# Rows of x scattered to the experts' slots, and TensorE's work in attention grouped by array form

## The chip, the cores and the metric

The kernel runs on one core of a Trainium2 chip. The metric is the device time of one execution in microseconds (us), lower is better. A profile is one execution recorded instruction by instruction; its times are counted from the start of its span. The core's engines are TensorE (PE in the profile, with its weight loads as PEld), VectorE (DVE), ScalarE (ACT), GpSimd (POOL) and SyncE (SP), which issues most transfers. Transfers run on 16 DMA engines. TensorE's clock has two levels, 1.2 and 2.4 GHz; the profile shows the granted clock as a share of the higher.

## The reference

Three layers follow each other. The first is a causal attention with decay, without softmax, over 4 batches of 576 positions and 8 heads of 64. The second is a mixture of 8 experts, each token going to two of them. The third is a dense layer with 2048 hidden units.

```python
scores = scale * np.matmul(q, k.transpose(0, 1, 3, 2))
ret = scores * Dmat                      # gamma_h ** (i - j) for j <= i, else 0
attn = np.matmul(ret, v)
x = attn.transpose(0, 2, 1, 3).reshape(2304, 512)

noisy = x @ w_gate + np.log1p(np.exp(x @ w_noise)) * noise
top2 = two largest of noisy;  top2_w = softmax over the two
out[mask] += top2_w * (np.maximum(x[mask] @ w1[e], 0) @ w2[e])   # for each expert e

h = out @ w_in
return (h * np.clip(h + 3, 0, 6) / 6) @ w_out
```

## The kernel before

Tokens are worked on in 18 tiles of 128 (`NT`). All instructions of an engine run in the order in which the program issues them; the order is written out by hand, and a wait holds everything behind it on the same engine or queue.

**Attention** runs over the tiles `t`. The state over earlier positions is kept as a 64x64 matrix per head (`pS`, copied into `sbd`), so that a tile needs only its own 128 keys. One turn of the loop in `attention` issues, in this order: the loads of tile t+3 on SyncE's queue (`load`, line 165), on some turns a piece of expert weights (`w_load`), the scaling of k and q of tile t+2 on VectorE (`ks`), the scores of tile t+1 on TensorE and their mask on VectorE (`qk`, lines 198 and 200), the gate sums and the rows of x of tile t-1 (`xt`, lines 254 and 259), the store of those rows to the DRAM tensor `xd` (`xstore`, line 221), the transposes of tile t+2 (`tr`, line 183), the output of tile t (`av`, line 211 for its own keys and line 215 for the state), the update of the state (`kv`, line 238), and the gate's logits of tile t-1 (`logit`, line 266).

TensorE's array takes these groups in four forms: line 198 uses half the rows (64x128, two at a time), lines 211 and 238 half the columns (128x64, two at a time), line 254 a quarter of the columns (128x32, four at a time), and lines 183, 215, 259 and 266 the full array (128x128).

**Routing.** Tiles are routed in groups of 4, 4, 4, 3 and 3. `route` is a generator; `rstep` runs its next step, five times in a turn of the loop, so that its short steps on VectorE, ScalarE and TensorE lie between the other work. One step counts with small matmuls (lines 325 to 328) which slot each token has in each of its two experts. The next scatters the tokens' ids with an indirect DMA of GpSimd's, two for each tile (line 344), into `tokd`, a DRAM table with a slot for each row of each expert; the table is filled with zeros at the start (line 140).

**Experts.** `moe` goes through sweeps: a run of an expert's slots against all eight hidden tiles. For each, `ix_load` reads the ids of the slots from `tokd` (line 572, SyncE), and `gather_x` gathers those rows of `xd` with indirect DMAs on GpSimd (line 589). `x_tile` transposes and splits a row tile (line 599), `g1` is the first matmul (line 620), `g2` the second (line 631). The first sweep (expert 0, 360 slots) needs only tokens of the first 12 tiles (`EARLY`); its rows are fetched at turn 15 (`GA`). The second sweep's rows are fetched at its hidden tile 5, when all tokens are routed. The output rows go to `yd`, and `moe2` gathers two for each token and runs the dense layer.

**Buffers.** Tags give rotating buffers: 32 of `big` (tiles of attention and weights), 13 of `row` (rows of x and y), 4 of `xa` (transposed rows of x), 5 accumulators in PSUM.

Of the kernel before, what the change touches and what calls it, by code (L numbers as in the profile page):

```python
# [7 lines left out]
F32 = mybir.dt.float32  # L8
F32R = mybir.dt.float32r
BF = mybir.dt.bfloat16  # L10
I32 = mybir.dt.int32
# [8 lines left out]
NT = N // 128  # L20
# [42 lines left out]
class K:  # L63
# [10 lines left out]
    # slots of one size, shared by all phases  # L74
# [20 lines left out]
    # ---------------------------------------------------------------- setup  # L95
# [23 lines left out]
    def late_consts(self):  # L119
# [11 lines left out]
        self.ids = cp.tile([P, NT], I32, name="ids")  # L131
        nc.gpsimd.iota(self.ids, pattern=[[P, NT]], base=0, channel_multiplier=1)
# [3 lines left out]
        nz = -(-E * REG // P)  # L136
        z = self.row([P, nz], I32)
        nc.gpsimd.memset(z, 0)
# [64 lines left out]
    def av(self, t):  # L203
# [9 lines left out]
        if m:  # L213
            for a in range(4):
                nc.tensor.matmul(px[:, a, :n], self.sbd[t % 2][:, a, :], r["qT"][:, a, :n], start=False,  # L215
                                 stop=True, skip_group_check=True)
        r["xT"] = self.row([P, 4, P])
# [27 lines left out]
    def xt(self, t):  # L245
        """rows of x, and the gate's sums over a quarter of the features each"""
# [4 lines left out]
        o = 256 + t % 2 * P  # L251
        pl = self.pg[:, o:o + P]
        for k in range(4):
            nc.tensor.matmul(pl[32 * k:32 * k + 32, :], self.wgn[:, k, :], r["xT"][:, k, :], start=True, stop=True)
        r["pl"] = self.sb.tile([P, P], F32, name="pl", bufs=2)
        nc.scalar.activation(r["pl"], pl, AF.Copy)
# [3 lines left out]
        r["x"] = self.row([P, DM])  # L260
        nc.scalar.activation(r["x"].rearrange("p (a d) -> p a d", a=4), p, AF.Copy)

    def logit(self, t):
        r = self.raw.pop(t)
        o = t % 8 * 16
        self.nc.tensor.matmul(self.pg[:, o:o + 16], r["pl"], self.c[:, C_FO:C_FO + 16], start=True, stop=True)

    # ---------------------------------------------------------------- route
    def route(self, g0, G):
# [52 lines left out]
        o = 128 + (g0 + 3) // 4 % 2 * 32  # L322
# [17 lines left out]
        for g in range(G):  # L340
            t = g0 + g
            for k in range(2):
# [28 lines left out]
    def late_base(self):  # L371
        """the late tokens of expert 0 start behind its first sweep"""
# [11 lines left out]
    def attention(self):  # L384
        self.raw = {}
# [20 lines left out]
        groups = [(0, 4), (4, 4), (8, 4), (12, 3), (15, 3)]  # L406
        assert EARLY in [g[0] for g in groups]
        self.live, self.sent = [], 0
        for t in range(NT):
# [17 lines left out]
            self.av(t)  # L427
# [5 lines left out]
            if t:  # L433
                self.gate(t - 1, groups)
            self.rstep()
            if t == GA:
                while self.sent < EARLY:
                    self.rstep()
                self.gather_x(0, 0)
            if t in WS:  # L440
                self.w_split()
            self.wstep(WN, eng=self.nc.gpsimd)
        for j in (1, 2):
            self.x_tile(0, xs, j, "acc" if j == 1 else "tp")
        self.xt(NT - 1)
        self.xstore(NT - 1)
# [3 lines left out]
    def gate(self, t, groups):  # L450
        self.logit(t)
# [6 lines left out]
    # ------------------------------------------------- weights, in f order  # L458
    # piece n: expert n // 4, pair of hidden tiles n % 4; from 32 on, moe2's
# [48 lines left out]
    def wstep(self, count=1, until=-1, eng=None):  # L508
        """the next parts of the split; all of piece `until`"""
# [6 lines left out]
    # ------------------------------ float64 weights to float32, chunk by chunk  # L516
# [41 lines left out]
    # ------------------------------------------------------------------ moe  # L558
    # a sweep: an expert's rows in one or two runs of slots, over all hidden tiles
# [3 lines left out]
    def run_of(e, r):  # L563
        """first slot, tiles, rows per tile"""
# [4 lines left out]
    def ix_load(self, e, r, n=1):  # L569
        o, T, R = self.run_of(e, r)  # L570
        t = self.tokd
        self.nc.sync.dma_start(self.ix[r][:R, e:e + n, :], bass.AP(
# [392 lines left out]
```

## Time and profile before

| what | us |
|---|---|
| median of 3 runs | 1035.94 (1035.67 to 1039.35) |
| span of the profiled execution, from its first to its last instruction | 1050.8 |
| what lies around the span in that execution | not listed |
| TensorE matmuls busy in the span | 1011.6 (96%) |
| weight loads | 893.3 (85%) |
| VectorE / ScalarE / GpSimd busy | 506.5 / 413.3 / 241.4 |

The profiled execution's only time is its span, which is 14.9 us longer than the median of the runs. TensorE is busy nearly all of the span, but the span has two parts: attention and routing up to about 205 us, where TensorE has gaps and its clock is at times at the lower level, and the experts and the dense layer behind, where it has next to none. Matmuls are pipelined and their ends are modelled, so starts are the safer measure. "Idle before" is the time for which an engine had nothing running ahead of an instruction, and behind the arrow stands what ended that; "issue" means nothing that the profile shows.

### The profile page before, as it was taken

Reading aid. Unit: us, or ns where it says so; the run is one execution under the profiler, and the core shown is the slowest. Engines: PE = TensorE matmul, PEld = TensorE weight load, DVE = VectorE, ACT = ScalarE, POOL = GpSimd, SP = SyncE. Lnnn points to the kernel's source line nnn. Section 1 sums busy time; section 2 is a strip of 40 time slices with the busy share of each in tenths; the row PEclk is TensorE's granted clock in tenths of the full one; section 3 lists DMA queues with packets and bytes.
Section 4 is the critical chain, followed back from the end, with each engine's and each line's share of the span. In section 5 each row is a group of like instructions: output and inputs, shape, how many; then the busy total and the mean of one; then the engine's idle time right before and its main releaser. Section 6 shows DMA issues by size and latency. Waiting matters only on the chain.

```text
span 1050.8 us, 16775 instructions
## 1 busy us (share of the span) xinstructions
PE 1011.6 (96%) x6370; PEld 893.3 (85%) x6370; DVE 506.5 (48%) x1178; ACT 413.3 (39%) x853; POOL 241.4 (23%) x299
## 2 busy tenths in 40 slices
PE   8988979799999999999999999999999999999996
PEld 5875768699889888898888989999999999999995
DVE  4545545166666666766766256332433333333221
ACT  4434542253434443343434246333433323333322
POOL 0035454402343524352423003110010010000000
PEclk9888879899999999999999999999999999999999
DMA  9878816664374747375545246211010020000000
GB/s 177 190 145 190 163 59 131 193 198 148 124 247 156 252 139 251 124 222 195 162 137 186 80 152 205 65 31 41 11 61 21 19 64 10 31 1 1 31 1 34
DMA packets 130863, 122.04 MB, mean 116 GB/s; under 512 B 68981, under 2 KB 98037, under 8 KB 130773
## 3 DMA queue, kind: packets, MB, share of 16 engines
q1 hardware_dynamic: 123541, 101.32, 34.4%
q0 software_dynamic: 7232, 19.56, 6.3%
q8 instruction: 52, 0.85, 0.4%
q14 instruction: 38, 0.31, 0.1%
HBM read 92.82 MB, written 28.02 MB: 115 GB/s over the span
## 4 chain that ended last, share of the span: by engine, by line
PE 88%; DMA 4%; DVE 2%; SPq 2%; issue 2%; POOL 1%; ACT 0%; another core or an unknown queue 0%; DVEq 0%; POOLq 0%
PE p L631 39%; PE ga L620 21%; PE gb L620 18%; PE xp L599 2%; DMA b<-in_q_dram 2%; PE px L215 1%; PE px L211 1%; SPq L165 1%; DMA b<-in_moe_w_dram 1%; PE sc L198 1%; PE p L183 1%; PE p L238 1%; PE p L259 1%; DMA tokd<-ids,slots 1%; POOL tokd L344 0%
## 5 line engine op out<-in xcount | busy, mean ns | idle before, releaser
L631 PE MATMUL p<-b,h 128*128 128x512 f32 (+1 forms) x1824 | 458.9, 397 | 0.0
L631 PEld LDWEIGHTS p<-b,h 128*128 128x128 f32 (+1 forms) x1824 | 331.4, 187 | 69.7 <-DVE h L668 0.3
L620 PE MATMUL ga<-x,b 128*128 128x360 f32 (+2 forms) x1344 | 235.1, 324 | 1.2 <-DVE h L668 1.2
L620 PEld LDWEIGHTS ga<-x,b 128*128 128x128 f32 x1344 | 218.4, 189 | 9.2 <-DVE h L668 1.9
L620 PE MATMUL gb<-x,b 128*128 128x384 f32 (+2 forms) x768 | 130.1, 318 | 0.0
L620 PEld LDWEIGHTS gb<-x,b 128*128 128x128 f32 x768 | 121.5, 188 | 4.3
L554 POOL TENSOR_TENSOR cvl<-cvl,cva 128x256 f32<-128x256 f32 x64 | 47.2, 738 | 214.8 <-ACT h L667 102.1
L729 POOL DMA_INDIRECT s<-yd,slotc x36 | 35.2, 979 | 253.5 <-DVE s L738 80.7
L620 PE MATMUL gb<-b,b 128*128 128x256 f32 x672 | 89.0, 281 | 0.0
L620 PEld LDWEIGHTS gb<-b,b 128*128 128x128 f32 x672 | 86.2, 189 | 0.5
L513 DVE TENSOR_TENSOR b<-b,b 128x512 fp32r<-128x512 f32 x112 | 79.7, 747 | 12.6 <-ACT b L512 11.9
L789 DVE SCALAR_TENSOR_TENSOR h<-h,h 128x384 fp32r<-128x384 f32 (+1 forms) x112 | 56.1, 501 | 61.1 <-ACT h L788 60.6
L512 ACT ACTIVATE b<-b 128x512 fp32r<-128x512 f32 x128 | 74.5, 623 | 14.9 <-PE p L631 11.9
L788 ACT ACTIVATE h<-h 128x384 fp32r<-128x384 f32 (+1 forms) x112 | 53.7, 479 | 63.7 <-DVE h L787 62.1
L787 DVE SCALAR_TENSOR_TENSOR h<-h,ga 128x384 f32<-128x384 f32 (+1 forms) x56 | 27.8, 497 | 96.3 <-ACT h L786 96.1
L787 DVE SCALAR_TENSOR_TENSOR h<-h,gb 128x384 f32<-128x384 f32 (+1 forms) x56 | 27.8, 497 | 95.4 <-ACT h L786 95.1
L786 ACT ACTIVATE h<-ga,three 128x384 f32<-128x384 f32 (+1 forms) x56 | 30.0, 535 | 99.9 <-PE ga L620 96.5
L786 ACT ACTIVATE h<-gb,three 128x384 f32<-128x384 f32 (+1 forms) x56 | 30.0, 535 | 89.8 <-PE gb L620 88.0
L668 DVE SCALAR_TENSOR_TENSOR h<-gb,h 128x256 fp32r<-128x256 f32 (+1 forms) x64 | 27.9, 435 | 71.5 <-PE p L631 41.2
L667 ACT ACTIVATE h<-ga 128x360 fp32r<-128x360 f32 (+1 forms) x64 | 29.3, 458 | 68.8 <-PE ga L620 66.6
L555 POOL TENSOR_TENSOR cvl<-cvt,cvl 128x256 f32<-128x256 f32 x64 | 54.9, 857 | 5.0
L344 POOL DMA_INDIRECT tokd<-ids,slots x36 | 35.8, 994 | 82.7 <-DVE rs L363 54.2
(129 smaller groups left out, 941.6 us busy)
## 6 DMA issues: line engine op xcount, KB each, us to landing
b<-in_moe_w_dram SPq DMA_DIRECT2D x64, 512.0 KB
s<-in_moe_w_in_dram SPq DMA_DIRECT2D x32, 256.0 KB
s<-in_moe_w_out_dram SPq DMA_DIRECT2D x32, 256.0 KB
yd<-s SPq DMA_DIRECT2D x24, 240.0 KB
xd<-s SPq DMA_DIRECT2D x18, 256.0 KB
out_dram<-s SPq DMA_DIRECT2D x18, 256.0 KB
b<-in_k_dram SPq DMA_DIRECT2D x16, 256.0 KB
b<-in_q_dram SPq DMA_DIRECT2D x16, 256.0 KB
```

Of the source, the lines that this page charges most:

```text
L344: st = nc.gpsimd.indirect_dma_start(out=self.tokd, out_offset=bass.IndirectOffsetOnAxis(ap=self.slots[:, t, k:k + 1], axis=0), in_=self.id ...
L512: self.nc.scalar.activation(h, a, AF.Copy)
L513: (eng or self.nc.vector).tensor_sub(l, a, h.bitcast(F32))
L554: nc.gpsimd.tensor_mul(lf, lf, a.bitcast(F32))
L555: nc.gpsimd.tensor_add(lf, t.bitcast(F32), lf)
L620: nc.tensor.matmul(p, a[:, k, f], b[:, k, :n], start=(i == 0), stop=(i == 11))
L631: nc.tensor.matmul(a[:R], x[:, c], y[:, fi, :], start=(first and i == 0), stop=(last and i == 2))
L729: nc.gpsimd.indirect_dma_start(out=r, out_offset=None, in_=self.yd[0:rows], in_offset=bass.IndirectOffsetOnAxis(ap=self.slotc[:, t, k:k + ...
L786: nc.scalar.activation(r, p, AF.Relu, bias=self.three)
L787: nc.vector.scalar_tensor_tensor(r, r, 6.0, p, op0=OP.min, op1=OP.mult)
L788: nc.scalar.activation(gh, r, AF.Copy, scale=1.0 / 6.0)
L789: nc.vector.scalar_tensor_tensor(gl, r, 1.0 / 6.0, gh.bitcast(F32), op0=OP.mult, op1=OP.subtract)
```

## The change

Two things are changed together.

Rows. The table of ids, its zero fill, the tensor `xd`, its 18 stores, the index loads and the 40 gathers of x go. Instead each tile's 128 rows of x are scattered from SBUF, once for each of the two experts of a token, into `xe`, a DRAM tensor with a 2 KB row for each slot. A sweep reads its rows from there with plain loads on SyncE's queue (`x_load`). The last 128 slots of each expert's first 616, and the last 128 of the first 360, are filled with zero rows at the start, from a tile of zeros.

Order. In a turn of the loop the full-array groups come first (rows of x of tile t-1, logits, transposes of tile t+2, line 215's group of tile t), then the 64-column groups (own keys and state), then the 64-row scores of tile t+1, and on every third turn the gate sums of three tiles at once (`gsum`). The scaling of k and q is issued at the end of a turn, for tile t+3. Routing groups become six of three tiles, and their logits are computed together.

```diff
-        self.tokd = self.dr.tile([P * nz, 1], I32, name="tokd")
-        nc.sync.dma_start(self.tokd.rearrange("(p f) o -> p (f o)", p=P), z)
...
-        self.xd = self.dr.tile([N, DM], F32, name="xd")
+        self.xe = self.dr.tile([E * REG, DM], F32, name="xe")
+
+        z = self.warm.bitcast(F32)
+        nc.sync.dma_start(self.xe.rearrange("(e r) d -> r e d", e=E)[CAP - P:CAP],
+                          z[:, None, :].to_broadcast([P, E, DM]))
+        nc.sync.dma_start(self.xe[NA - P:NA], z)
...
+        if m:
+            for a in range(4):
+                nc.tensor.matmul(px[:, a, :n], self.sbd[t % 2][:, a, :], r["qT"][:, a, :n], start=(a == 0),
+                                 stop=False, skip_group_check=True)
+        self.px = px
+
+    def av2(self, t):
+        nc, m = self.nc, t % 9
+        r, px = self.raw[t], self.px
         for a in range(4):
             for s in range(2):
                 h = slice(s * 64, s * 64 + 64)
-                nc.tensor.matmul(px[h, a, :], r["v"][:, 2 * a + s, :], r["pt"][:, s, a, :], start=(a == 0),
-                                 stop=(m == 0), skip_group_check=True)
...
+                nc.tensor.matmul(px[h, a, :], r["v"][:, 2 * a + s, :], r["pt"][:, s, a, :],
+                                 start=(m == 0 and a == 0), stop=True, skip_group_check=True)
+        g = t // 3
+        if t % 3 == 0:
+            self.xg[g] = self.act_t([P, 4, 3 * P], F32)
+        r["xT"] = self.xg[g][:, :, t % 3 * P:t % 3 * P + P]
         nc.scalar.activation(r["xT"], px, AF.Copy)
-
-    def xstore(self, t):
-        self.nc.sync.dma_start(self.xd[t * P:(t + 1) * P, :], self.raw[t]["x"])
...
+    def gsum(self, g):
+
+        nc = self.nc
+        p = self.pacc([P, 3 * P])
+        x = self.xg.pop(g)
+        for k in range(4):
+            nc.tensor.matmul(p[32 * k:32 * k + 32, :], self.wgn[:, k, :], x[:, k, :], start=True, stop=True)
+        self.pl = self.sb.tile([P, 3 * P], F32, name="pl", bufs=2)
+        nc.scalar.activation(self.pl, p, AF.Copy)
...
-                    out=self.tokd, out_offset=bass.IndirectOffsetOnAxis(ap=self.slots[:, t, k:k + 1], axis=0),
-                    in_=self.ids[:, t:t + 1], in_offset=None)
+                    out=self.xe, out_offset=bass.IndirectOffsetOnAxis(ap=self.slots[:, t, k:k + 1], axis=0),
+                    in_=x, in_offset=None)
...
+        self.ks(2)
+        groups = [(g, 3) for g in range(0, NT, 3)]
...
-            if t + 2 < NT:
-                self.ks(t + 2)
-            if t + 1 < NT:
-                self.qk(t + 1)
+
             if t:
                 self.xt(t - 1)
-                self.xstore(t - 1)
+            if t > 3 and t % 3 == 1:
+                self.gate(t - 2, groups)
             self.rstep()
             if t + 2 < NT:
                 self.tr(t + 2)
+            self.av(t)
             self.rstep()
             self.wstep(WM, eng=self.nc.gpsimd)
-            self.av(t)
+
+            self.av2(t)
             self.kv(t)
             self.rstep()
...
-            if t:
-                self.gate(t - 1, groups)
+            if t + 3 < NT:
+                self.ks(t + 3)
+
+            if t + 1 < NT:
+                self.qk(t + 1)
+            if t and t % 3 == 0:
+                self.gsum(t // 3 - 1)
             self.rstep()
...
+    def x_load(self, e, r):
+
         o, T, R = self.run_of(e, r)
...
+        xv = self.xe[e * REG + o:e * REG + o + T * R].rearrange("(p j) d -> p j d", j=T)
         for j in range(T):
             x = self.row([P, DM])
-            nc.gpsimd.indirect_dma_start(
-                out=x[:R], out_offset=None, in_=self.xd[0:EARLY * P] if (e, r) == (0, 0) else self.xd,
-                in_offset=bass.IndirectOffsetOnAxis(ap=self.ix[r][:R, e, j:j + 1], axis=0))
+            self.nc.sync.dma_start(x[:R], xv[:, j, :])
             self.xr[e, r, j] = x
```

## Rows read from the trace of the kernel before

**Rows 1.** Busy time by stretch: length, each engine's busy time, clock, DMA share, GB/s.

```profile
205.00:1043.30 838.30, 836.33 (x4723) 750.03 (x4721) 412.36 (x874) 331.66 (x673) 169.82 (x193) 1.00 0.34 108
27.40:148.60 121.20, 107.20 (x1183) 87.78 (x1183) 58.50 (x185) 57.50 (x131) 49.12 (x66) 0.87 0.73 156
```

**Rows 2.** TensorE's timeline over one tile: start, length, line, tiles, shape, count.

```profile
37.59 0.69 PE L238 MATMUL p<-b 128*64 128x64 f32 x16
38.20 0.40 PE L266 MATMUL p<-cst,pl 128*128 128x16 f32 x2
38.53 1.16 PE L198 MATMUL sc<-b 64*128 64x128 f32 x16
39.62 0.42 PE L254 MATMUL p<-s,wgn 128*32 128x128 f32 x8
39.98 0.66 PE L259 MATMUL p<-cst,s 128*128 128x128 f32 x4
40.47 1.04 PE L183 MATMUL p<-cst,b 128*128 128x128 f32 x8
41.44 1.09 PE L211 MATMUL px<-b,b 128*64 128x128 f32 x16
42.46 1.10 PE L215 MATMUL px<-b,s 128*128 128x64 f32 x8
43.49 0.68 PE L238 MATMUL p<-b 64*64 64x64 f32 x16
```

**Rows 3.** TensorE's waits, 20 to 150 us: us in total, times, longest.

```profile
PE px L215 <- issue: 4.8, 7, 1.0
PE px L211 <- issue: 3.8, 11, 0.5
...
PE p L238 <- issue: 1.7, 2, 0.9
```

**Rows 4.** GpSimd's indirect DMAs by line: ns shortest, median, longest; first and last start.

```profile
L344 POOL DMA_INDIRECT tokd<-ids,slots x36: 954/958/1297, 55.6 to 179.3; - x36
...
L589 POOL DMA_INDIRECT s<-xd,ixa x24: 973/1016/1457, 143.4 to 575.9; - x24
```

**Rows 5.** Busy time by stretches of 5 us, columns as in rows 1.

```profile
65.00:70.00 5.00, 3.47 (x31) 3.20 (x33) 0.00 (x0) 2.68 (x6) 0.82 (x1) 0.62 0.28 60
...
105.00:110.00 5.00, 5.00 (x36) 4.33 (x36) 1.29 (x2) 2.78 (x6) 2.50 (x2) 0.50 0.99 43
...
130.00:135.00 5.00, 2.99 (x23) 1.89 (x22) 1.40 (x3) 0.28 (x1) 4.13 (x9) 0.95 0.02 0
...
160.00:165.00 5.00, 5.00 (x28) 4.55 (x27) 3.87 (x21) 1.06 (x5) 2.32 (x6) 1.00 0.87 199
```

**Rows 6.** The chain that ended last, behind attention: start, length, what.

```profile
179.26 5.33 DMA tokd<-ids,slots
185.03 4.22 DMA ixa<-tokd
191.18 3.49 DMA s<-xd,ixb
```

**Rows 7.** TensorE's timeline: instructions that waited, the wait in brackets.

```profile
26.35 1.09 PE L183 MATMUL p<-cst,b 128*128 128x128 f32 x4 [0.72 <-DVE b L173]
...
151.70 0.17 PE L328 MATMUL p<-ra,tri 128*128 128x8 bf16 x1 [3.13 <-DVE ra L318]
...
193.46 1.09 PE L599 MATMUL p<-cst,s 128*128 128x128 f32 x4 [6.87 <-DMA s<-xd,ixb]
```

**Rows 8.** Busy time in one us with a store of x, columns as in rows 1.

```profile
36.00:37.00 1.00, 1.00 (x16) 0.83 (x11) 0.25 (x1) 0.28 (x1) 0.00 (x0) 1.00 0.82 260
```

**Rows 9.** TensorE's timeline in windows that begin inside a group.

```profile
40.25 0.38 PE L259 MATMUL p<-cst,s 128*128 128x128 f32 x2
...
40.69 0.82 PE L183 MATMUL p<-cst,b 128*128 128x128 f32 x6
```

**Rows 10.** SyncE's queue: issues of line 221, start and length.

```profile
143.12 14.38 SPq L221 DMA_DIRECT2D xd<-s  x3
```

More of the change, by code (lines that the diff above doesn't have):

```diff
@@ L130, in late_consts @@
         nc.vector.memset(self.macc, 0.0)
-        self.ids = cp.tile([P, NT], I32, name="ids")
-        nc.gpsimd.iota(self.ids, pattern=[[P, NT]], base=0, channel_multiplier=1)
         self.slots = cp.tile([P, NT, 2], I32, name="slots")
@@ L210, in av @@
                 h = slice(s * 64, s * 64 + 64)
-                nc.tensor.matmul(px[h, a, :], r["v"][:, 2 * a + s, :], r["pt"][:, s, a, :], start=(a == 0),
-                                 stop=(m == 0), skip_group_check=True)
[L213 to L217, printed above, removed]
+                nc.tensor.matmul(px[h, a, :], r["v"][:, 2 * a + s, :], r["pt"][:, s, a, :],
[4 more added lines that the diff above has]
+        r["xT"] = self.xg[g][:, :, t % 3 * P:t % 3 * P + P]
         nc.scalar.activation(r["xT"], px, AF.Copy)
-    def xstore(self, t):
-        self.nc.sync.dma_start(self.xd[t * P:(t + 1) * P, :], self.raw[t]["x"])
     def kv(self, t):
@@ L250, in xt @@
             self.pg = self.pacc([P, 512])
[L251 to L256, printed above, removed]
         p = self.pacc([P, 4, P])
@@ L259, in xt @@
             nc.tensor.transpose(p[:, a, :], r["xT"][:, a, :], self.ident)
-        r["x"] = self.row([P, DM])
-        nc.scalar.activation(r["x"].rearrange("p (a d) -> p a d", a=4), p, AF.Copy)
+        self.xrow[t] = self.row([P, DM])
+        nc.scalar.activation(self.xrow[t].rearrange("p (a d) -> p a d", a=4), p, AF.Copy)
+    def gsum(self, g):
[6 more added lines that the diff above has]
+        nc.scalar.activation(self.pl, p, AF.Copy)
     def logit(self, t):
-        r = self.raw.pop(t)
+        self.raw.pop(t)
         o = t % 8 * 16
-        self.nc.tensor.matmul(self.pg[:, o:o + 16], r["pl"], self.c[:, C_FO:C_FO + 16], start=True, stop=True)
+        j = t % 3 * P
+        self.nc.tensor.matmul(self.pg[:, o:o + 16], self.pl[:, j:j + P], self.c[:, C_FO:C_FO + 16],
+                              start=True, stop=True)
     def route(self, g0, G):
@@ L321, in route @@
             yield
-        o = 128 + (g0 + 3) // 4 % 2 * 32
+        o = 128 + g0 // 3 % 2 * 32
         pr = self.pg[:, o:o + G * 8].rearrange("p (g e) -> p g e", g=G)
@@ L341, in route @@
             t = g0 + g
+            x = self.xrow.pop(t)
             for k in range(2):
@@ L384, in attention @@
     def attention(self):
-        self.raw = {}
+        self.raw, self.xrow = {}, {}
         self.consts()
@@ L405, in attention @@
         self.late_consts()
-        groups = [(0, 4), (4, 4), (8, 4), (12, 3), (15, 3)]
+        self.ks(2)
+        groups = [(g, 3) for g in range(0, NT, 3)]
         assert EARLY in [g[0] for g in groups]
-        self.live, self.sent = [], 0
+        self.live, self.sent, self.xg = [], 0, {}
         for t in range(NT):
@@ L438, in attention @@
                     self.rstep()
-                self.gather_x(0, 0)
+                self.xr = {}
+                self.x_load(0, 0)
             if t in WS:
@@ L442, in attention @@
             self.wstep(WN, eng=self.nc.gpsimd)
+        self.gsum(NT // 3 - 1)
         for j in (1, 2):
@@ L445, in attention @@
         self.xt(NT - 1)
-        self.xstore(NT - 1)
         self.gate(NT - 1, groups)
@@ L450, in gate @@
     def gate(self, t, groups):
-        self.logit(t)
+        for u in range(t - 2, t + 1):
+            self.logit(u)
         for g0, G in groups:
@@ L567, in run_of @@
         return (0 if e == E - 1 else NA), 2, RB
-    def ix_load(self, e, r, n=1):
+    def x_load(self, e, r):
         o, T, R = self.run_of(e, r)
-        t = self.tokd
-        self.nc.sync.dma_start(self.ix[r][:R, e:e + n, :], bass.AP(
-            tensor=t.tensor, offset=t.offset + e * REG + o, ap=[[T, R], [REG, n], [1, T]]))
-    def gather_x(self, e, r):
-        nc = self.nc
-        if (e, r) == (0, 0):
-            self.ix = (self.cp.tile([P, E, 3], I32, name="ixa"), self.cp.tile([P, E, 2], I32, name="ixb"))
-            self.xr = {}
-            self.ix_load(0, 0)
-        if (e, r) == (0, 1):
-            self.ix_load(0, 1, E - 1)
-            self.ix_load(1, 0, E - 2)
-            self.ix_load(E - 1, 0)
-            self.ix_load(E - 1, 1)
-        _, T, R = self.run_of(e, r)
+        xv = self.xe[e * REG + o:e * REG + o + T * R].rearrange("(p j) d -> p j d", j=T)
         for j in range(T):
             x = self.row([P, DM])
-            nc.gpsimd.indirect_dma_start(
-                out=x[:R], out_offset=None, in_=self.xd[0:EARLY * P] if (e, r) == (0, 0) else self.xd,
-                in_offset=bass.IndirectOffsetOnAxis(ap=self.ix[r][:R, e, j:j + 1], axis=0))
+            self.nc.sync.dma_start(x[:R], xv[:, j, :])
             self.xr[e, r, j] = x
@@ L693, in moe @@
                     for s in nxt:
-                        self.gather_x(*s)
+                        self.x_load(*s)
                         xs[s] = self.x_new(s[1])
@@ L866, in rest_body @@
                 r0 = i * P + (e * REG + CAP)
-                ix = self.sb.tile([P, 1], I32, name="rix")
-                nc.sync.dma_start(ix, self.tokd[bass.ds(r0, P), :])
                 x = self.row([P, DM])
-                nc.gpsimd.indirect_dma_start(out=x, out_offset=None, in_=self.xd,
-                                             in_offset=bass.IndirectOffsetOnAxis(ap=ix[:, 0:1], axis=0))
+                nc.sync.dma_start(x, self.xe[bass.ds(r0, P), :])
                 p = self.ps.tile([P, 4, P], F32, name="tp")
@@ L936, in body @@
             nc = tc.nc
-            for n, a in dict(slots=k.slots, gw=k.gw, xd=k.xd, tok=k.tokd).items():
+            for n, a in dict(slots=k.slots, gw=k.gw).items():
                 if n in dbg:
```

3 lines of the change are left out of this document (removed).

## Prediction

> **What bounds the kernel now.** I read the stretches first, then the chain of waits, then TensorE's timeline in the early part. From 205 us to 1043 us TensorE is busy 836.3 of 838.3 us at a granted clock of 1.00 (2.4 GHz) [rows 1]. Nothing that the change touches can shorten that stretch, and the loads that it moves there (from GpSimd's queue to SyncE's) have a DMA share of 0.34 around them. What can move is the first 205 us. In the stretch 27.4 to 148.6, sixteen attention tiles, TensorE is busy 107.2 of 121.2 us, at a clock of 0.87, with the DMA engines at 0.73 [rows 1]. The timeline of an undisturbed tile shows its pace: the matmuls of line 238 start at 37.59 and again at 43.49, so 5.90 us [rows 2]. Sixteen such tiles are 94.4 us; some 27 us of the stretch are lost to waits and to the lower clock level.
>
> Where they are lost: TensorE's largest waits there are put down to "issue", nothing that the profile shows: 4.8, 3.8 and 1.7 us before the groups of lines 215, 211 and 238 [rows 3]. They stand beside the bursts of scatters. GpSimd scatters token ids from 55.6 us on, 36 times at 0.96 us [rows 4]. Around three of these bursts the engine runs few matmuls, then is at 1.2 GHz for a while (0.62 in 65 to 70, 0.50 in 105 to 110), and in 105 to 110 the DMA engines are busy 0.99 of the time for 43 GB/s [rows 5]. I put about 24 of the 27 us to these three places; the rest stands at the first wait below.
>
> Behind attention the chain of waits runs in DMA steps: the last scatter is issued at 179.26 and takes 5.33 us to land, the index loads 4.22 us, the gather of rows 3.49 us [rows 6]. TensorE waits 6.87 us for it at 193.46 [rows 7].
>
> **The base.** The profiled execution's span is 1050.8 us and the median of the runs 1035.94, 14.9 below it. I sum differences and take them from the median. Where the 14.9 us lie is not shown.
>
> **The change, term by term.**
>
> *Zero rows.* The fill of the id table (84 KB) goes; nine blocks of 128 rows of 2 KB come, 2.36 MB, ahead of the loads of tile 4 on SyncE's queue. The window 36 to 37, in which 256 KB rows are stored, has 260 GB/s at a share of 0.82 [rows 8]: 9.1 us at that rate, 7.4 at a full share. TensorE already waits for tile 4's q and k there (0.72 us at 26.35) [rows 7], so nothing covers the fill. Bounds 3 (if some goes beside other transfers) and 9; I take +6.5, near the full share, less the old fill. Everything queued behind it on SyncE's queue, from tile 4's k on, comes later by that.
>
> *Groups by form.* Inside a form a 128x128 matmul starts every 0.11 us: two of line 183 lie between 40.47 and 40.69 [rows 2, 9]. Eight would be 0.87 us, but the next form starts 0.97 after the first, 0.10 more. At the other end, line 259's third matmul starts 0.27 after its first, not 0.22: 0.05 more [rows 2, 9]. So a change of form costs 0.15 us. A tile now has seven: 64-row scores, 32-column gate sums, full, 64-column, full (line 215), 64-column, full (line 266), and back [rows 2]. The new order has full, 64-column, 64-row, and every third tile 32-column: 3.3. That is 3.7 x 0.15 = 0.55 us a tile, 8.8 for the sixteen tiles behind the first wait (those ahead of it only wait longer). Bounds 0, if another thing paces attention, and -9.9 for all eighteen; I take -8.8. The scores are now computed just ahead of the transposes of the next tile; those and line 215's group (0.49 + 0.97 + 1.09 us [rows 2]) hide the mask on VectorE. If VectorE is late by more, line 211's group waits next.
>
> *Gate sums and routing groups.* Eighteen sums of 128 columns become six of 384, the same columns. Five routing groups become six, about ten small matmuls more: +0.5.
>
> *Scatters.* The number stays 36, GpSimd's time too: a gather of such rows takes 1.0 us, a scatter of ids 0.96 [rows 4]. What the trace of before doesn't show is a scatter of rows. The stalls by the scatters may go wholly (-24, as beside the nearest rows in kind, stored rows, TensorE is busy throughout [rows 8]) or stay (0, as beside the nearest rows in place, the ids). The profiled execution is 14.9 above the median, and if that excess is these stalls, only 24 - 15 = 9 are there to be had in a timed run. I take -9. The bytes: 24 scatters of 256 KB in place of 15 stores within the stretch, 2.4 MB more, 9 us of DMA time at 260 GB/s, against a share of 0.73 in 121.2 us, 33 us free [rows 1, 8]. Bounds 0 and +9; I take +2.
>
> *Stores of x go from SyncE's queue.* Three of them hold it from 143.12 for 14.38 us [rows 10], with weight loads behind. The loads of tiles and weights then start when their buffers are free. I cost it at nothing by itself; it helps cover the last term. In the sweeps up to five loads of rows an expert join that queue ahead of weight loads and of stores. One that waits for its buffer holds those, where a gather held GpSimd's work. At a DMA share of 0.34 and TensorE's 836 of 838 us [rows 1] there is slack for it: nothing. Without it, the split of the weights and then line 620 come late.
>
> *The end of attention.* TensorE waits 3.13 us at 151.70 for VectorE's routing steps [rows 7]. In the new order that group's steps come after the first g1 of the sweep, where other matmuls stand ahead. -3 (0 to -3.1). What is late next is that group's scatter, by a few us, which only the next sweep needs.
>
> *The first sweep's end.* Last scatter, index load, gather becomes last scatter, load. The scatter as before (5.33) or as the gather of the same bytes (3.49) [rows 6]; the last group's scatter step stands one g1 later, but weights arrive earlier. A plain load of 256 KB has no row; it lies between 1.0 us (the rate of rows 8) and 4.22 (an index load, rows 6); I take 3. Then the rows are there near 188 in place of 193.5, and much of the low clock behind the wait goes too. -6 (bounds -2 and -9.5).
>
> Sum: 6.5 - 8.8 + 0.5 - 9 + 2 - 3 - 6 = -17.8, so 1035.9 - 17.8 = 1018.
>
> **Rivals.**
>
> 1. The stalls come with any scatter of GpSimd's, whatever its size. For it: no trace here has a scatter without them in attention. Against it: in 160 to 165, with GpSimd scattering, TensorE is busy throughout at 1.00 [rows 5], though there on long matmuls. Then the stall term is 0, the bytes +3, the last term -4: -5.8, 1030.
>
> 2. The stalls go wholly and are in timed runs too: stalls -24, last term -9: -35.8, 1000. What speaks for it is the landing of 512 bytes in 5.33 us against 3.49 for 256 KB [rows 6], so small writes land worse than large reads. The Trainium skill, "DMA: Bandwidth & Descriptors", Specifications, says that below 512 B the DMA engines read, modify and write; by that rule the ids' 4 bytes are the cause, and this rival's 1000 would be the time.
>
> 3. Slower: the DMA engines become attention's bound. Work there is 0.73 x 121.2 = 88 us; with 9 for rows and 7 for zeros it is 104 [rows 1, 8]. It decides from where the engines run slower than now by about 15%, as they did in 105 to 110 at 43 GB/s [rows 5]. If each of four bursts of rows has 5 us at 43 GB/s in place of 260, four of the five are lost, so +16; the gain by form is hidden (0), the stalls stay (0): 6.5 + 16 + 0.5 - 3 - 4 = +16, 1052. The Trainium skill, "DMA: Bandwidth & Descriptors", Issuing engines are not separate DMA queues, says that all queues end on the same engines; by that the move to another queue frees nothing, and this rival stands.
>
> 4. The gain by form is eaten by VectorE: the scaling of tile t+3 stands ahead of the mask and waits for loads, so line 211 waits each tile. Form term 0, else as forecast: -9, 1027.
>
> 5. As 4, with the stalls left: 6.5 + 0.5 + 3 - 3 - 6 = +1, 1037, no change.
>
> **Numbers.** Forecast 0.34; rivals 0.18, 0.18, 0.10, 0.12, 0.08. Time 1018. Range 998 to 1033: it takes in the forecast, rivals 1, 2 and 4, and leaves out 3 and 5 (0.18). A measurement tells about 0.5% from no change, that is 5.2 us: below 1030.8 is faster. Faster: forecast, 2, 4 and half of rival 1, with a little for bounds, 0.75. Same: 0.13. Slower: 0.12.
>
> **What would show it.** Right: tile 4's transposes start some 6 us later; an undisturbed tile takes 5.3 to 5.4 us; no "issue" waits beside the scatters; the first wait of the sweep behind attention under 3 us; from there on all as before. Wrong: the same "issue" waits and the slow DMA stretches by scatters of rows; a DMA share near 1 from 30 us on with line 183 waiting for k and q; line 211 waiting for masks; a wait in the dense part for rows.

## Result, and the profile after

On the chip where both were timed first, the changed kernel takes 1021.3 us (1020.48 to 1022.65, four runs) and the kernel before 1037.64: a ratio of 0.9843, 95% interval 0.9818 to 0.9867, so 16.3 us less. The forecast was 1018 and 17.8 less. The time of the kernel before differs by chip; that of the changed one did not where it ran: in two later comparisons, on two chips, the changed kernel took 1020.79 and 1021.55, and the kernel before 1036.22 (ratio 0.984, 0.9811 to 0.9869) and 1047.41 (0.9739, 0.9702 to 0.9776). The profile shown of before has a span of 1050.8, longer than any of its timed runs here (1035.67 to 1039.81); on which chip it was taken is not on record. Times below are therefore compared on one chip, and stretches by profiles.

Where the time went is read best from four landmarks of TensorE's timeline: the first transposes of tile 4 (lines 183 / 181), the first matmul of the experts (620 / 622), the first transposes that the second sweep does for the third (599 / 601, the column "2nd sweep"), and the span. The fifth column is the granted clock in 27.4 to 148.6 us, the stretch of [rows 1]. Times in us.

| profile | tile 4 | 1st sweep | 2nd sweep | span | clock |
|---|---|---|---|---|---|
| before, shown above | 24.89 | 156.60 | 211.59 | 1050.8 | 0.87 |
| after | 31.20 | 139.94 | 185.66 | 1020.9 | 0.89 |
| before, one chip (g1) | 24.83 | 150.22 | 203.58 | 1043.3 | 0.91 |
| after, the same chip (g2) | 30.64 | 138.44 | 184.14 | 1019.5 | 0.90 |
| rows only (e2) | 30.28 | 157.37 | 201.23 | 1042.6 | 0.84 |
| order only (e3) | 24.76 | 156.68 | 213.26 | 1047.5 | 0.82 |
| after, zero rows late (h2) | 24.44 | 149.27 | 194.99 | 1029.6 | 0.88 |
| after, scatters spread (f2) | 30.70 | 128.86 | 174.57 | 1009.1 | 0.95 |
| after, split on VectorE (f3) | 30.48 | 128.84 | 177.09 | 1012.2 | 0.92 |
| after, all three (f4) | 24.34 | 123.45 | 169.16 | 1004.1 | 0.99 |
| before without scatters (h1) | 25.19 | 124.62 | 168.48 | 1006.5 | 0.98 |

From the first line to the second, tile 4 comes 6.3 later; from there to the first sweep takes 108.7 in place of 131.7; from the first sweep to the transposes in the second 45.7 in place of 55.0; from there to the end 835.2 in place of 839.2. That is +6.3, -23.0, -9.3 and -4.0, together -29.9, the difference of the spans (the sums are of rounded numbers). On one chip, from g1 to g2, the four are +5.8, -17.6, -7.7 and -4.4.

Busy time by stretch, after, to be held against [rows 1]:

```profile
205.00:1013.00 808.00, 804.86 (x4554) 725.33 (x4553) 395.52 (x847) 317.82 (x644) 137.24 (x164) 1.00 0.33 105
27.40:148.60 121.20, 105.75 (x1204) 92.32 (x1205) 82.08 (x261) 61.14 (x139) 49.86 (x71) 0.89 0.83 216
```

The long stretch is TensorE's as before. In the other the DMA share has risen from 0.73 to 0.83; no tile of attention keeps TensorE waiting for loads after tile 4. TensorE's timeline, line 241 (the state's update, line 238 before), three tiles from 41.71 on:

```profile
41.71 0.63 PE L241 MATMUL p<-b 128*64 128x64 f32 x16
...
48.38 0.68 PE L241 MATMUL p<-b 64*64 64x64 f32 x16
...
53.36 0.63 PE L241 MATMUL p<-b 128*64 128x64 f32 x16
...
58.61 0.64 PE L241 MATMUL p<-b 128*64 128x64 f32 x16
```

That is 16.90 us for three tiles with one set of gate sums, 5.63 a tile, and 4.98 for a tile without them. Three tiles of the kernel before, undisturbed, in its profile g1 (below), take 18.21 us, 6.07 a tile:

```profile
36.58 0.69 PE L238 MATMUL p<-b 128*64 128x64 f32 x16
...
54.79 0.69 PE L238 MATMUL p<-b 128*64 128x64 f32 x16
```

TensorE's waits, 20 to 150 us, after:

```profile
PE p L181 <- DVE b L169: 10.4, 2, 7.8
PE p L337 <- DVE ra L327: 5.6, 1, 5.6
PE xp L601 <- DMA s<-xe: 1.9, 1, 1.9
PE p L181 <- DVE b L171: 1.0, 1, 1.0
```

The "issue" waits of [rows 3] are gone. The second line is a new one, of 5.56 us, and the timeline around it (all engines) tells where it comes from:

```profile
83.05 7.39 POOL L531 TENSOR_TENSOR b<-b,b 128x512 fp32r<-128x512 f32 x6
...
84.30 6.19 DVE L302 TENSOR_TENSOR rln<-rln,ru 128x24 f32<-128x24 f32 x1
...
92.36 0.17 DVE L327 TENSOR_TENSOR ra<-rm 128x24 bf16<-128x24 bf16 x1
...
92.58 0.17 PE L337 MATMUL p<-ra,tri 128*128 128x8 bf16 x1 [5.56 <-DVE ra L327]
```

VectorE's subtraction of 24 columns (line 302) takes 6.19 us. It ends as GpSimd's row of six weight splits (line 531) ends, and TensorE's count of slots waits for what follows it. The splits had piled up there: GpSimd issued six scatters one behind the other from 75.28 to 82.93, and the splits stood behind them in its queue. The same happens twice more, to line 293 (4.20 us at 105.58 and 3.16 at 131.88), so that two operations of the routing take over 1 us in the mean (by line, form and count; busy us, mean ns):

```profile
L293 DVE TENSOR_SCALAR rw<-ru 128x24 f32<-128x24 f32 x6 | 8.1, 1345 | 7.1 <-ACT ru L290 7.0
L302 DVE TENSOR_TENSOR rln<-rln,ru 128x24 f32<-128x24 f32 x6 | 7.1, 1178 | 0.2
```

Such a wait costs twice, since the clock falls behind it. Stretches of 5 us, after, columns as in [rows 1]:

```profile
65.00:70.00 5.00, 5.00 (x74) 4.69 (x72) 4.41 (x21) 3.17 (x8) 1.70 (x4) 1.00 1.09 357
80.00:85.00 5.00, 5.00 (x71) 4.69 (x70) 3.87 (x9) 3.98 (x11) 4.44 (x7) 1.00 0.93 302
90.00:95.00 5.00, 2.42 (x25) 2.18 (x25) 4.04 (x23) 2.48 (x6) 0.48 (x2) 0.61 1.00 228
110.00:115.00 5.00, 2.85 (x14) 2.60 (x15) 4.83 (x15) 2.87 (x6) 3.24 (x3) 0.66 0.00 0
```

Without a wait the clock stays at 1.00, with the DMA engines at 0.93 or more. In the stretches in which the waits of 5.56 and 2.52 us end (at 92.6 and 111.2) it is 0.61 and 0.66.

### The profile page after: what moved, and what is told of

Its sections match the earlier page's. It is cut to its first block, busy times and chain, and to the rows that moved or that the text cites. A ratio compares the mean times of both kernels' runs of the same rounds, so it can differ in the third digit from the quotient of the medians.

```text
span 1020.9 us, 16506 instructions
## 1 busy us (share of the span) xinstructions
PE 985.3 (97%) x6268; PEld 880.9 (86%) x6268; DVE 515.6 (51%) x1203; ACT 411.9 (40%) x845; POOL 197.4 (19%) x257
## 4 chain that ended last, share of the span: by engine, by line
PE 87%; DMA 5%; DVE 4%; SPq 1%; issue 1%; POOL 1%; ACT 1%; DVEq 0%; POOLq 0%; ACTq 0%
PE p L633 38%; PE ga L622 21%; PE gb L622 19%; DMA yd<-s 2%; PE xp L601 2%; PE px L218 1%; PE sc L196 1%; PE p L181 1%; DMA s<-in_moe_w_out_dram 1%; PE px L208 1%; DMA b<-in_k_dram 1%; DVE rw L293 1%; SPq L163 1%; PE p L256 1%; DVE rln L302 1%
## 5 line engine op out<-in xcount | busy, mean ns | idle before, releaser
L633 PE MATMUL p<-b,h 128*128 128x512 f32 (+1 forms) x1824 | 451.2, 393 | 0.0
L354 POOL DMA_INDIRECT xe<-s,slots x36 | 36.4, 1011 | 102.8 <-DVE rs L373 57.9
```

Source lines behind the costliest of these rows:

```text
L354: st = nc.gpsimd.indirect_dma_start(out=self.xe, out_offset=bass.IndirectOffsetOnAxis(ap=self.slots[:, t, k:k + 1], axis=0), in_=x, in_off ...
L633: nc.tensor.matmul(a[:R], x[:, c], y[:, fi, :], start=(first and i == 0), stop=(last and i == 2))
```

## Experiments

The kernels of one row of letters (e, f, g, h) ran on one chip each, four chips in all, and ratios are to the kernel before there. Which kernel ran where matters below: e2, e3 and e4 ran only on the chip of row e, h2 only on that of row h, and the changed kernel itself on neither.

**e1: the kernel before again.** No edit.

> The kernel before, profiled once more. The profiled execution of before had a span of 1050.8 us, about 13 above the median of its runs, while the changed kernel's span (1020.9) and median (1021.3) agree. If the stalls beside the scatters of ids vary from execution to execution, and that one had them at their worst, the span is now 1034 to 1038 and TensorE's waits put down to issue between 27 and 150 us are half of the 10 us seen, or less. If they belong to every profiled execution of this kernel, the span is 1048 to 1053 again, with the same waits.

1046.52 us (span 1044.6, between the two ranges expected), where the runs of the kernel before on that chip have a median of 1049.07 (1045.3 to 1055.75). Its TensorE has "issue" waits too: 6.9 us before line 211, 2.4 before 215, 1.6 and 1.2 before 183 and 238. So the pauses were no accident of the first profile: an execution that takes the usual time of this chip has them.

**e2: rows only.** The rows part on the order of before.

```diff
-                    out=self.tokd, ... in_=self.ids[:, t:t + 1], in_offset=None)
+                    out=self.xe, ... in_=x, in_offset=None)
...
-            nc.gpsimd.indirect_dma_start(out=x[:R], ... in_=self.xd ...)
+            nc.sync.dma_start(x[:R], xv[:, j, :])
```

> The kernel before with the rows scattered and loaded back, its order of TensorE's work and its routing groups unchanged. My theory: zero rows +6.5, stalls -9, bytes +2, first sweep's end -6, so about 6 below before, 1028 to 1034. Rival, the rows are all of the gain: 1021. Rival, the order is all of it, and what rows save the zero rows take: 1036 to 1040.

1042.87 us, ratio 0.9933 (0.9911 to 0.9955): 6.2 less, the size that was expected, but not by the terms that were expected. The gain lies behind attention: from the first sweep to the transposes in the second it is 43.9 us, 53.4 in g1 and 55.0 in the first profile. The pauses stay, beside scatters of 2 KB rows. The timeline of one of them (TensorE, GpSimd, ScalarE):

```profile
62.69 0.43 PE L249 MATMUL p<-s,wgn 128*32 128x128 f32 x8
...
65.72 0.96 POOL L340 DMA_INDIRECT xe<-s,slots  x1 [0.22 <-issue]
66.22 0.47 PE L208 MATMUL px<-b,b 128*64 128x128 f32 x4 [0.99 <-issue]
...
66.99 0.96 POOL L340 DMA_INDIRECT xe<-s,slots  x1 [0.22 <-issue]
67.22 0.27 PE L208 MATMUL px<-b,b 128*64 128x128 f32 x1 [0.54 <-issue]
...
69.39 0.27 PE L208 MATMUL px<-b,b 128*64 128x128 f32 x1 [1.09 <-issue]
...
72.36 0.28 ACT L251 ACTIVATE pl<-p 128x128 f32<-128x128 f32 x1 [9.04 <-issue]
```

While GpSimd issues its eight scatters, TensorE starts one or two matmuls of 0.27 us at a time and waits 0.5 to 1.1 us in between. ScalarE's copy of the gate sums starts at 72.36, though the matmuls of line 249 had their start at 62.69. So the size of what is scattered is not the cause. How busy the DMA engines are does not decide it either. In this pause they are busy throughout (66 to 72, columns as in [rows 1]); in the pause of the kernel before at 130 to 135 their share is 0.02 [rows 5].

```profile
66.00:72.00 6.00, 1.98 (x10) 1.00 (x10) 2.58 (x4) 0.00 (x0) 4.03 (x7) 0.87 1.06 360
```

The Trainium skill's rule on writes below 512 B ("DMA: Bandwidth & Descriptors", Specifications) can't explain these pauses, as no row that these scatters write is under 2 KB.

**e3: order only.** The other part alone; ids are scattered, x is stored and gathered as before.

> The changed kernel with the ids scattered, x stored and gathered as before; order of TensorE's work and routing groups as changed. My theory: the form term alone, now put at 0.43 us a tile, so -7 to -8, and the wait at the end of attention -3: 1026 to 1030, with the waits put down to issue still there beside the scatters. Rival, the order is worth nothing alone because the stalls set the pace: 1035 to 1038. Rival, the order is all of the gain: 1021.

1047.61 us, ratio 0.9975 (0.9955 to 0.9995), nearer to the rival, by which the order alone is worth nothing, than to the theory. Between 20 and 150 us TensorE waits 17.5 us in three places for ScalarE's copy `pl`, and 5.0 us for "issue". The gain of the order is there tile by tile (three undisturbed tiles, from 35.44 to 52.34, take 16.90 us as in after), and goes into the pauses: from tile 4 to the first sweep 131.9 us, as in the profile of before. On this chip the parts alone give 6.2 and 1.5 us; on three others both together give 15 to 26. How much of that difference is the chips' is not known.

**e4 and h2: the changed kernel with its zero rows later.** The two stores of zeros move from the setup into turn 5 of the loop. The same kernel ran twice, on two chips.

```diff
+            if t == 5:
+                self.zero_rows()
```

> The changed kernel with the zero rows written at turn 5 of the attention loop, behind the loads of tile 8, in place of ahead of the loads of tile 4. My theory: the wait of 7.8 us before the transposes of tile 4 falls to about 2, and nothing else waits for the fill: 6 below the changed kernel, 1014 to 1016. Rival, the time is given back at a later wait (VectorE held up, a load that is late behind the fill): 1019 to 1022.

> The changed kernel with its zero rows stored in the sixth tile, a second time. Theory (the changed kernel escapes the pauses by where its bursts meet TensorE's groups; 6.3 us earlier they meet them elsewhere): pauses of 5 to 7 us beside one to three bursts as in the first run of it, 1027 to 1034, ratio 0.981 to 0.990 where the kernel before takes 1045 to 1050. Rival (the pauses of that run belonged to its chip): none here, 1010 to 1016.

1031.5 us, ratio 0.9839 (0.9805 to 0.9872), and 1031.82 us, 0.9807 (0.9768 to 0.9845); that is 10 us slower than the changed kernel's 1021 on its three chips, and slower than either side of e4 expected. Tile 4 comes 6.2 us earlier, and pauses as in e3 take more than that back. They are the same on both chips: TensorE's three waits for the copy `pl` sum to 18.1 us in e4 and 18.0 in h2. One of them in h2 (all engines):

```profile
51.40 0.63 PE L244 MATMUL p<-b 128*64 128x64 f32 x16
...
51.70 1.13 POOL L357 DMA_INDIRECT xe<-s,slots  x1 [50.71 <-DVE rs L376]
...
53.05 0.85 PE L269 MATMUL p<-x,wgn 128*32 128x384 f32 x8
...
54.23 5.91 SPq L166 DMA_DIRECT2D b<-in_v_dram  x1
...
60.34 0.49 ACT L271 ACTIVATE pl<-p 128x384 f32<-128x384 f32 x1 [5.73 <-remote]
...
60.88 1.46 PE L277 MATMUL p<-cst,pl 128*128 128x16 f32 x6 [6.39 <-ACT pl L271]
```

Line 269's matmuls run at 53.05; ScalarE's copy of their result starts at 60.34, and TensorE waits 6.39 us for it. One issue of SyncE, beside them, takes 5.91 us; but one of 5.06 (at 55.28 in f4) and one of 4.49 (at 54.83 in f1, ahead of any scatter) go with no pause. GpSimd's six scatters go from 51.70 to 59.15.

So a kernel that differs from the changed one only in the place of two stores has pauses. That the shift of 6 us brings them on is not shown: f4 (below) has the same shift, on another chip, and no pause. And the same burst in after meets TensorE at the same place and does no harm:

```profile
58.91 1.13 POOL L354 DMA_INDIRECT xe<-s,slots  x1 [57.92 <-DVE rs L373]
...
61.19 0.49 ACT L268 ACTIVATE pl<-p 128x384 f32<-128x384 f32 x1 [1.05 <-PE p L266]
```

In both profiles the burst begins 0.30 us behind the start of the state's update (line 244 at 51.40 here, line 241 at 58.61 there), yet the copy `pl` starts 8.64 us behind the burst's first scatter here and 2.28 there. In e3 and e4, which have the pause, and in f1, g2, f3 and f4, which do not, the first burst stands in the same place to 0.01 us. What does separate them is the chip: each profile of the new order that shows pauses is from the chips of rows e and h, and each that shows none is from the first chip or those of rows f and g. So the chip is a rival that no run here excludes.

**f1, g1, g2: both kernels again.** No edits.

> The changed kernel once more, unchanged. Theory A (the pauses beside the bursts of scatters depend on which of TensorE's instructions meet the burst, and the order of both parts together happens to escape them): again no wait of TensorE marked 'issue' and none on ACT pl over 2 us between 20 and 150 us of the span, span 1017 to 1023, ratio 0.982 to 0.987. Rival B (the pauses belong to the execution or to the chip, and the changed kernel was only lucky where it ran first): pauses of 5 to 7 us beside one to three bursts, span 1026 to 1036, while the ratio still holds if the kernel before has its own pauses here.

> The kernel before, unchanged, for a profile beside the changed kernel's on one chip. Theory A (its pauses of TensorE beside the scatters belong to its order of work): waits marked 'issue' of 5 to 15 us in all between 20 and 150 us wherever it runs, and a granted clock in that stretch below 0.90. Rival B (the pauses belong to the chip, and go with its time of 1049 on one chip against 1036 on another): none where the kernel before takes 1034 to 1040, and 8 to 15 us where it takes 1045 to 1056.

> The changed kernel, unchanged, on the chip of the run before this one. Theory A (its order of work escapes the pauses): no pause beside a scatter, 1018 to 1023, whatever the kernel before takes there. Rival B (the pauses belong to the chip): where the kernel before takes 1034 to 1040 the changed kernel takes 1019 to 1023 without pauses; where it takes 1045 to 1056, the changed kernel shows pauses too and takes 1028 to 1036.

f1: 1020.79 us, g2: 1021.55 us, no pause beside a scatter in either, and the same three waits as in the first profile of after (5.6 us for line 327 in both). g1: 1045.13 us. It has no "issue" waits, which both theories got wrong for a chip like this; it waits for VectorE's scaling of k and q instead, 17.3 us, 2.5 of them at tile 4:

```profile
PE p L183 <- DVE b L173: 9.3, 4, 3.6
PE p L183 <- DVE b L171: 8.0, 3, 5.5
PE xp L599 <- DMA s<-xd,ixa: 6.6, 2, 6.2
```

VectorE in its turn waits for loads of k and q, and two of SyncE's issues near the second burst (83.80 to 93.6) take 4.86 and 8.09 us:

```profile
87.95 4.86 SPq L165 DMA_DIRECT2D b<-in_v_dram  x1
...
96.79 8.09 SPq L165 DMA_DIRECT2D b<-in_q_dram  x1
```

The longest in after is 3.91 (4.49 in f1). These waits differ from the pauses of e1: most stand behind a burst and not beside it, and beside the third burst of g1 (122.35 to 132.4) TensorE has no wait. That the scatters cause them is not shown by g1 alone. Since g1 shows no pause of e1's kind, g2 without pauses does not tell either whether the order or the chip spares the changed kernel.

**h1: the kernel before without scatters.**

```diff
-        nc.gpsimd.memset(z, 0)
+        nc.gpsimd.iota(z, pattern=[[1, nz]], base=0, channel_multiplier=1)
...
-                st = nc.gpsimd.indirect_dma_start(out=self.tokd, ... in_=self.ids[:, t:t + 1], ...)
```

> The kernel before without its 36 scatters of row numbers; the table of row numbers that the experts read back is filled once at the start (row p + f), so the experts work on other rows and only the time counts. Everything else, the gate's sums, GpSimd's splits and SP's queue, stays. Theory (the pauses of the attention come from the bursts of eight scatters): no wait marked 'issue' beside a former burst, no issue of SP that takes over 3 us between 50 and 130 us, and 0.978 to 0.988 of the kernel before. Rival (the pauses come from SP's queue, where each tile's store of x stands ahead of the next loads): SP's issues still take 4 to 8 us, TensorE still waits, and the time is within 0.5% of the kernel before.

1010.64 us, where the kernel before takes 1052.98: 42 us less, a ratio of 0.96 (0.9563 to 0.9636), and more than either side had expected. The stretch of attention in g1 (on another chip) and in h1:

```profile
27.40:148.60 121.20, 99.10 (x1209) 83.04 (x1212) 63.24 (x210) 60.26 (x136) 50.14 (x68) 0.91 0.75 160
```

```profile
27.40:148.60 121.20, 117.86 (x1353) 100.85 (x1353) 76.67 (x275) 66.06 (x152) 34.22 (x54) 0.98 0.79 209
```

TensorE is busy 117.9 us in place of 99.1, at a clock of 0.98. No issue of a load takes over 2.8 us between 50 and 117 us. The stores of x are not faster: two from 102.25 on take 7.57 us and three from 117.13 on 8.42, so that what was expected of SyncE's issues holds for the loads alone. Some of the 42 is not the pauses: GpSimd's splits no longer stand behind scatters, and no sweep waits for one. From tile 4 to the first sweep it is 26 us (125.4 in g1, 99.4 here), with 6.6 us of g1's wait for the first rows (line 599) in it.

**f2: scatters spread.** In the changed kernel, a tile's two scatters are issued once in each turn of the loop, not six in one step of the routing.

```diff
+            self.scatter()      # two of the scatters that are due
             self.av2(t)
```

> The changed kernel, with the scatters of a group of three tiles no longer issued as six in a row, but two for each attention tile (the same 36 scatters, the same addresses). Theory (what hurts is the length of the run of scatters on GpSimd: it holds the splits behind it together in bundles of 4 to 6, beside which VectorE's small instructions were held 4.2 and 6.2 us): with two scatters (2.5 us) in each tile, the splits leave GpSimd two at a time, the VectorE instructions beside them are held 2.5 us at most, and TensorE's waits of 5.56 and 1.86 us shrink: 1014 to 1019, ratio to the changed kernel 0.994 to 0.998, and no pause of over 3 us beside a scatter even where the changed kernel shows some. Rival C (only the number of scatters counts, or the splits alone): within 0.3% of the changed kernel. Rival D (rows stay longer in their buffers, so loads start later and the splits come between scatters of the last groups): 1023 to 1028.

1012.71 us, ratio 0.9763 (0.9739 to 0.9787), 8.1 us better than f1 on the same chip, and more than was expected. A scatter goes as soon as its slots are there and what stands ahead of it in GpSimd's queue is done, so that the edit only changes what stands next to what there: in the second and third group the splits now come two at a time between pairs of scatters. The other groups still go six in a row.

```profile
81.44 0.98 POOL L373 DMA_INDIRECT xe<-s,slots  x1
...
82.73 1.24 POOL L373 DMA_INDIRECT xe<-s,slots  x1 [0.21 <-issue]
84.04 2.50 POOL L537 TENSOR_TENSOR b<-b,b 128x512 fp32r<-128x512 f32 x2
...
86.74 0.98 POOL L373 DMA_INDIRECT xe<-s,slots  x1 [0.15 <-issue]
```

The two operations of VectorE are at 0.45 and 0.33 us in place of 1.35 and 1.18, TensorE's longest wait for line 327 is 1.4 in place of 5.6, and the clock of the stretch 0.95.

**f3: the splits on VectorE.**

```diff
-            self.wstep(WN, eng=self.nc.gpsimd)
+            self.wstep(WN)
```

> The changed kernel, with the subtractions that split the experts' weights issued on VectorE instead of GpSimd during attention. Theory (VectorE's small instructions were held because GpSimd's subtractions had the memory port that both share): the instructions of 4.2 and 6.2 us fall back to 0.2 us, TensorE's waits of 5.56, 2.5 and 1.9 us on the routing's results go, at the price of 24 or so subtractions of about 0.6 us more on VectorE: 1012 to 1017. Rival E (VectorE's small instructions were held by something else beside them, such as the scatters' descriptors): they stay over 2 us and the time is within 0.3% of the changed kernel. Rival F (VectorE has no room in the attention, as its work of a tile is near the pace): the tiles get longer, 1024 to 1028.

1009.57 us, ratio 0.9727 (0.9702 to 0.9752), 11.2 us better than f1, again more than was expected. The operations are short again:

```profile
L302 DVE TENSOR_TENSOR rln<-rln,ru 128x24 f32<-128x24 f32 x6 | 1.1, 179 | 0.6 <-DVE ru L297 0.5
...
L293 DVE TENSOR_SCALAR rw<-ru 128x24 f32<-128x24 f32 x6 | 1.1, 176 | 4.7 <-ACT ru L290 4.6
```

The Trainium skill gives a reason in "SBUF — State Buffer", Who interferes with whom: a VectorE instruction with two inputs in SBUF and a GpSimd instruction that reads SBUF exclude each other, and the second to come waits until the first has ended. The trace agrees on who is held; but line 302, which started as the second of the six splits did, was held through five of them, not through one of 1.23 us. Line 293 has one input, so this sentence does not cover it, though f3 frees it too. The wait of 1.86 us that the expectations count with these is for the first load of rows; it stays (2.7 us in f2, 3.0 in f3).

**f4: all three.** Zero rows in turn 5, scatters by turns, splits on VectorE.

> The changed kernel with all three: the zero rows stored in the sixth tile instead of ahead of the loads, two scatters for each tile instead of six in a row, the weights' subtractions on VectorE. Theory (the 6.3 us of the first loads come back if no pause takes them, and the routing's waits go too): 1004 to 1012, ratio to the kernel before 0.968 to 0.976. Rival G (what is won ahead of the first tile is given back later whatever the scatters do, since another limit sets the end of the attention, such as the loads of q, k, v and the experts' weights): 1016 to 1022, with TensorE waiting on loads instead.

1006.9 us, ratio 0.9711 (0.9684 to 0.9738): the fastest version, 13.9 us better than the changed kernel on that chip and 29 better than the one before. With no splits between them, GpSimd issues the scatters six in a row as in after (from 50.19, 51.62, 52.90 us on), and yet there is no pause; no profile of this chip shows one. What TensorE still waits for, 20 to 180 us:

```profile
PE p L340 <- DVE ra L330: 3.6, 3, 1.4
PE xp L612 <- DMA s<-xe: 3.2, 1, 3.2
PE p L184 <- DVE b L174: 2.6, 4, 1.0
```

Against f3 the zero rows' 6.1 us are won at tile 4, 5.4 are left at the first sweep and 2.7 in the medians, which the intervals don't tell apart. The first load of rows (3.22 us) is late next.

## Why the prediction was right in its number, and where not

*Zero rows, +6.5*: right, +6.3. But a later store of the zeros alone does not win it back on the chips of rows e and h (e4, h2).

*Groups by form, -8.8*: right in kind, too large. A tile takes 5.63 in place of 6.07, so 0.44 and not 0.55, and the 5.3 to 5.4 us that were to show it are not reached. It comes with the order alone (e3). If all of it is the 3.7 changes of form less, that is 0.12 us for one, not 0.15, and -7.0 for sixteen tiles; no run parts the forms from the rest of the order. No plain tile waits for VectorE, so rival 4 falls.

*Scatters, -9*: this is the step that failed. It took the 14.9 us between the first profile and the runs for pauses of that execution alone, and the rest for a gain that comes with larger rows. But e1 shows pauses in an execution of the usual time of its chip, and with e2 they stay beside rows of 2 KB. So on that chip rival 1's mechanism is right, rival 2's is wrong, and h1 shows on another that without scatters there are none. Yet rival 1's 1030 was not the time: the three profiles of the changed kernel show no such pauses. Whether its order spares it or its chips do is not shown, since the parts (e2, e3) and the kernels closest to it (e4, h2) ran on other chips.

The size: between the first two profiles the way from tile 4 to the first sweep is 23.0 us shorter; less 7.0 for the form and 1.2 for the end of attention that leaves about 15 for the scatters. In the timed runs it was less. Of the 16.3 us there, the other terms as the profiles have them (+6.3, -7.0, -1.2, -7.7 to -9.3, -4.0) make 13.6 to 15.2, so that 1 to 3 are left, an estimate, as no profile of before is known to be from that chip. Both are net of a wait that was not foreseen and that the sum put at nothing: VectorE's operations held beside the splits, worth 8 to 11 us by f2 and f3. By this estimate 9 to 14 us were won at the scatters in the timed runs, not far from the 9, and most of it was lost again to that wait. That the sum came out near all the same is luck: -4.0 in the stretch that was to stay as before, 1.7 to 3.3 more at the first sweep's end and 2 less for bytes made up for it.

*Bytes, +2*: no tile of attention waits for loads behind tile 4, so nothing. Rival 3's share of 1 is not reached in the mean of the stretch (0.83), and rows land in 5.7 us (issue to landing, from the page of after):

```profile
s<-xe SPq DMA_DIRECT2D x24, 240.0 KB, 5.7
```

*The end of attention, -3*: -1.2. The wait of 3.13 us for routing [rows 7] is gone, and the first load of rows is late next, where the text had named the last group's scatter:

```profile
134.95 0.60 PE L601 MATMUL xp<-cst,s 120*128 120x120 f32 x4 [1.86 <-DMA s<-xe]
```

From the end of tile 17's last group to the first sweep it is 6.8 us, 8.0 before.

*The first sweep's end, -6*: -9.3 between the two first profiles and -7.7 between g1 and g2, inside its bounds. The rows took 5.7 and not 3 us to land; the wait of 6.87 us [rows 7] is gone all the same: the last scatter is issued at 163.74, and line 601's transposes at 170.71 wait for nothing.

*From there on all as before*: not quite; -4.0 us. All kernels with the new order take 834 to 835 us from the transposes in the second sweep to the end, all others 838 to 841. The second matmul's mean (by line and form; busy us, mean ns) is 396 in e2 and 392 in e3 and after:

```profile
L610 PE MATMUL p<-b,h 128*128 128x512 f32 x1105 | 283.6, 396 | 0.0
```

```profile
L652 PE MATMUL p<-b,h 128*128 128x512 f32 x1104 | 279.2, 392 | 0.0
```

```profile
L633 PE MATMUL p<-b,h 128*128 128x512 f32 x1134 | 286.4, 392 | 0.0
```

So it comes with the order part. Why is open.

Open, too: why the changed kernel and f4 run through bursts of six scatters without a pause, while e3, e4 and h2, with bursts as long, do not. For the first burst it is not the place in TensorE's work at which it comes, which is the same in all of them. The chips differ, and the changed kernel on the chip of row e or h, which would tell, was not run. Through what the scatters hold TensorE and ScalarE the profile does not show. No profile was taken of the kernel before on a chip where it is known to take 1036 us, so how much of its time there is pauses is not known.

## What to carry to other kernels

Look at what stands behind a run of scatters in GpSimd's own queue: two scatters and two splits in turn cost 8 us less here than six and six, at the same count. Where two parts of a change act on the same pauses, measure them together and apart, all on one chip: 6.2 and 1.5 us on one chip stand here beside 15 to 26 on three others, and what the order adds cannot be told from what the chip does. And count a wait of TensorE with the clock behind it: the stretch of 5 us in which the wait of 5.56 us ended ran at 0.61.

## What the runs showed of the hardware

A burst of six to eight indirect scatters (0.96 us each, 1.27 apart) can hold other engines: TensorE to steps of about 1 us (e2), and ScalarE by 5.7 (h2) to 9.0 us (e2). It does so with 4 bytes and with 2 KB a row, at a DMA share of 0.02 and of 1.06, and it does not always do so: all profiles with scatters from two chips show it, and none from two others. A VectorE operation of 0.18 us took 6.19 beside five subtractions of GpSimd in a row. The kernel before takes 1036 to 1053 us on four chips, by their medians; the changed one, which shows no such pauses, 1020.8 to 1021.6 in three comparisons.
